# The order of the side steps in the first up stage of a retention and SwiGLU kernel, laid out anew

## The chip, the core and the metric

The kernel runs on one core of one Trainium2 chip. The metric is the device time of one execution in microseconds (us); the number for a kernel is the median of several executions. Five engines work side by side on the core, each through its own list of instructions in order: TensorE (PE in the profile), VectorE (DVE), ScalarE (ACT), GpSimd (POOL), and SyncE (SP), which here only issues transfers (DMA). An instruction that has to wait holds up everything behind it in the list of its own engine.

## What is computed

```python
# retention, for B=4 sequences, H=8 heads, S=768 tokens, head size D=64
for t in range(S):
    state = gamma * state + k[t] (outer) v[t]
    y[t]  = scale * q[t] @ state
x = y as (3072 tokens, 512)
# SwiGLU block, d_ff = 1536
g   = x @ w_gate
val = x @ w_val
out = (silu(g) * val) @ w_out
```

The three weight matrices arrive as 8-byte words, so the kernel first turns them into 4-byte floats. This can be seen in the sizes of the loads: the 512 x 256 values that one step of the up stage needs come as 1 MB.

## The kernel before, in words

The 3072 tokens are taken in four segments of 768 (two sequences, three chunks of 128 tokens each). Each segment has an up stage, in which both `x @ w_gate` and `x @ w_val` are formed, and a down stage, which multiplies by `w_out`. The retention of the first segment comes before everything (the string `START`); that of each later segment is woven into the down stage before it. The hidden dimension of 1536 is cut into 12 blocks of 128, counted by f.

**The first up stage** is what the change is about: `up(f)`, lines 654 to 702, called for f = 0 to 11. The gate and value blocks are treated as one 2 x 2 block product and formed with seven products where eight would be plain, each of 128 x 384 results and two contracted blocks (line 664, two full-precision matmuls, four records in the trace). For this, weights and inputs are first added and subtracted. For one f the list of PE is:

- B11 into bank x (bank 0 for even f, 1 for odd f), then T4 of the f before into the other x bank (`gates`, line 673), then T1 into bank 2, T2 into x, B22 into bank 2, T3 into x, B21 into bank 3.
- ACT copies x after B11 (line 683), runs the two Silu of the f before (lines 675 and 676), copies bank 2 after T1 (line 688) and x after T2 (line 691). B22 and T3 add to what stands in their banks and therefore wait for these copies.
- DVE adds after B22 (line 694), after T3 (line 697) and after B21 (line 700). The addition of line 697 reads x, so T4 of this f, which adds to x in the next f, waits for it. `muls` (lines 679 and 680) multiply by the gate and free the x bank for the f after next.

**The side steps.** Between these products the kernel prepares the weights for later f and for the down stage, and stores them in DRAM for the segments to come. The list `beside`, indexed by `6 * f + place`, is the table of places: `aside(f, place)` issues the steps written there. Place 0 stands after T4, place 1 after T1 and its copy, 2 after T2 and its copy, 3 after B22 and its addition, 4 after T3 and its addition, 5 after B21 and its addition. Nothing but this table (and waits on data) decides where a side step stands in the list of its engine. `START` is such a list for the work ahead of f = 0. The letters, with n the number of a weight piece (0 to 11: up, block f = n; 12 to 23: down, blocks 3 to 11 and then 0, 1, 2):

- `Un:w` loads a piece into raw space w (SP, line 191; three transfers for an up piece, 1 MB, one for a down piece, 512 KB). Raw space: `rawp0` to `rawp3` hold one up piece or two down pieces each, the front of `loads` two down pieces more.
- `an`, `cn`, `bn` convert on ACT: a (line 209) the upper words, c (line 217) the lower words, b (line 213) the signs into PSUM banks, two of 512 columns for an up piece and one for a down piece. `Sn` (DVE, line 223) joins signs and words, `Cn` (POOL, line 232) adds the lower words. Cn needs Sn and cn; Sn needs bn.
- `Tn:0`, `Tn:1`, `Tn:2` (DVE, line 80) form T1 and T3, T2, and T4 of up piece n; Tn:0 needs Cn.
- `Fn:0` to `Fn:3` split a down piece into three parts of lower precision: ACT (line 728), POOL (line 731), DVE (line 734), DVE (line 738). The parts lie in one of three slots.
- `Zn` stores a prepared piece (SP, line 160 for up, 249 for down), `Mf` is `muls` of f, `Ln` and `Pn` load tables and q, k, v for the later retention (SP; L is four or five small transfers), `gn` decays a retention state (ACT, four instructions, line 445), `tn`, `kn` work on the state and on k.

The list of SP is in order too. Each transfer waits, besides for its data, for the one issued eight before it to have landed, since eight counters are used in turn.

**Later stages.** `WHEN` holds times at which steps of the other stages are issued in program order; `('u', 0)` to `('u', 3)` are those of `up3`, the up stage of segments 1 to 3, for f = 0, 1, 2 to 10, and 11.

Of the kernel before, what the change touches and what calls it, by code (L numbers as in the profile page):

```python
# [24 lines left out]
NF = DFF // P  # L25
L = 3
TH = L * P
NSEG = B * NCK // (2 * L)
# [21 lines left out]
def tile_retnet_swiglu(  # L50
# [69 lines left out]
    def at(t, fn, *args, **kw):  # L120
        events.append((t, len(events), lambda: fn(*args, **kw)))
# [30 lines left out]
    T3, B22, B12, T1, B11, B21, T2, T4 = 0, 1, 2, 2, 3, 4, 5, 6  # L152
# [131 lines left out]
    def do(order):  # L284
        for o in order.split():
# [6 lines left out]
        l0:0 l0:1 A0 A1 l1:0 l1:1 l0:2 l1:2 A2 l0:3 l2:0 l2:1 l1:3 l2:2 l2:3 l3:0 l3:1 l3:2  # L292
        l3:3 l4:0 l4:1 U0:0 l4:2 l5:0 l5:1 l5:2 U1:2 l4:3 l5:3 s0 w6 s1 m0 m1 K0 t0 K1 s2 t1
        g2 g3 Q2 s3 m2 x0:0 x0:1 x0:2 x0:3 k2 q3 t2 s4 a0 b0 m3 k3 t3 q4 c0 s5 S0 x1:0 x1:1
        x1:2 x1:3 m4 a1 q5 C0 U2:0 m5 x2:0 T0:0 x2:1 T0:1 x2:2 x2:3 T0:2 U3:4 U12:6
    """
    beside = """
        b1 | c1 S1 U13:7 | g5 g4 C1 | a2 T1:0 U14:8 | U15:9 | c2 b2 T1:1 a3 |
        S2 T1:2 | b3 C2 Z0 S3 | Z1 T2:0 | c12 c3 a12 C3 M0 b12 | U5:0 a13 T2:1 | T2:2 |
        S12 C12 T3:0 M1 |  | T3:1 F12:0 U4:2 Z2 | T3:2 a4 b4 U6:4 S4 a5 Z3 | F12:1 c4 F12:2  # L300
            C4 | b5 S5 T4:0 |
        T4:1 c6 L0 | M2 U16:6 c5 C5 | b13 c13 S13 | L1 C13 U7:2 a6 a14 | F12:3 T5:0 U8:0 b6
            | T4:2 T5:1 S6 F13:0 |
        F13:1 Z4 F13:2 b14 | F13:3 Z13 C6 M3 S14 | a15 a7 b7 c7 | T5:2 T6:0 T6:1 Z12 | S7
            T6:2 Z5 L3 c14 b15 | C14 U18:8 F14:0 |
        S15 C7 F14:1 | M4 F14:2 F14:3 | a8 U9:4 U17:7 Z6 c15 | C15 a16 Z14 | L2 F15:0 T7:0 |
            F15:1 c8 b8 |
        T7:1 S8 | U10:2 F15:2 a9 M5 C8 F15:3 | a17 T7:2 c16 b16 | U19:9 T8:0 b9 | U11:0 S16
            P0 C16 S9 F16:0 | P1 b17 |
        F16:1 T8:1 F16:2 Z15 c9 | T8:2 F16:3 Z7 | a10 Z16 S17 c10 C9 | c17 M6 C17 | U22:4  # L310
            a19 U20:6 F17:0 T9:0 a18 F17:1 | T9:1 b10 |
        k4 Z8 U21:7 b18 | S10 C10 a11 F17:2 S18 | M7 U23:5 c18 F17:3 | T10:0 T9:2 | b19 Z9
            b11 C18 F18:0 | T10:1 F18:1 F18:2 S11 P2 c19 Z17 c11 |
        T10:2 S19 F18:3 M8 a20 | b20 C11 | c20 S20 | a21 b21 T11:0 | a22 S21 C19 C20 | T11:1
            T11:2 t4 c21 Z18 F19:0 |
        F19:1 F19:2 k5 F20:0 Z10 F19:3 | b22 F20:1 t5 C21 a23 b23 | F21:0 S22 c22 M9 F21:1
            Z11 F20:2 | c23 F20:3 C22 Z19 | S23 F22:0 C23 F21:2 | F21:3 Z20 |
        F23:0 F22:1 Z21 F22:2 | M10 F22:3 Z22 | F23:1 F23:2 |  | F23:3 | |
        Z23
    """.split("|")  # L320
    sign_banks = {0: (0, 1), 1: (4, 5), 3: (4, 6), 12: (7,), 19: (4,), 20: (7,), 21: (6,), 22: (7,), 23: (6,), 4: (6, 7), 5: (6, 7), 6: (6, 7), 7: (6, 7), 8: (6, 7), 9: (6, 7), 10: (6, 7), 11: (6, 7), 13: (4,), 14: (4,), 15: (4,), 16: (4,), 17: (4,), 18: (4,), 2: (6, 7)}

# [2 lines left out]
    WHEN = {  # L325
        ('u', 0): (1.15, 2.16, 2.86, 3.39, 4.9, 5.3, 8.05, 13.63, 7.4, 8.1),
        ('u', 1): (0.41, 2.51, 3.16, 3.92, 4.38, 5.59, 6.95, 8.3, 7.26, 12.66),
        ('u', 2): (0.33, 1.32, 3.61, 3.15, 4.0, 5.51, 5.85, 6.13, 7.28, 7.66),
        ('u', 3): (1.63, 1.81, 3.34, 2.86, 3.53, 5.07, 6.18, 7.14, 7.05, 7.54),
        ('w', 0, 0): (-11.39, -6.27, -4.75),  # L330
        ('w', 0, 1): (-7.89, -7.84, -1.53),
        ('w', 0, 2): (-10.42, -10.31, -9.95),
        ('w', 1, 0): (-9.1, -4.79, -3.1),
# [47 lines left out]
        'end': (1.36, -0.0, 0.1, 1.03, 7.96, 4.59),  # L381
        'last': (0.1, 0.1, 0.1, 0.1, 0.1, 0.1),
        ('h', 12): (-7.5, -6.3, -5.3),
    }

    UP0, T0 = 9.45, 18.0
# [420 lines left out]
    def weights(t, f, g):  # L807
        it = {}

        def begin():  # L810
            it["o"] = group(f, g)
            near_a(*it["o"])

        a, b, c = WHEN["w", min(f, 2), g]
        at(t + a, begin)
        at(t + b, lambda: near_b(*it["o"]))
        at(t + c, lambda: near_c(it["o"][0]))
# [11 lines left out]
    def up3(s, f, t):  # L829
        x, z, wb = (banks[i][:, :TH] for i in (6 + f % 2, 0, 1))  # L830
        p1, u2, p5 = (tmp[:, ts(i, TH)] for i in range(3))
        c11 = tmp[:, ts(3 + f % 2, TH)]
        gate = banks[2 + f % 2][:, :TH]
        for g, first in enumerate((0, 3, 6)):
            weights(t + first * PROD, f, g)
        for n, p in enumerate(ORDER):
            o = {1: x, 6: x, 7: x, 4: x, 2: z, 5: wb, 3: wb}[p]
            at(t + n * PROD, product, s, f, p, o, p in (1, 2, 5))
        h0, h1 = hT[:, f, 0], hT[:, f, 1]
        steps = (lambda: copy(p1, x), lambda: tt(c11, z, p1, op=add),  # L840
                 lambda: act(gate, c11, AF.Silu, scale=ONE), lambda: copy(u2, x),  # L841
                 lambda: copy(p5, wb), lambda: tt(h1, x, p5, op=add),  # L842
                 lambda: tt(h0, wb, u2, op=add), lambda: tt(h0, h0, gate, op=mul),  # L843
                 lambda: act(x, x, AF.Silu, scale=ONE), lambda: tt(h1, h1, x, op=mul))  # L844
        for d, step in zip(WHEN["u", 3 if f == NF - 1 else min(f, 2)], steps):
            at(t + d, step)


# [144 lines left out]
    for s in range(1, NSEG):  # L993
        for f in range(NF):
            up3(s, f, t + UPT * f)
            if f > 2:
                at(t + UPT * (f - 1) - 2.5, load_unit, f)
        t += NF * UPT
        if s + 1 < NSEG:
            for n in range(5):  # L1000
                at(t - (18, 13, 12, 5, 4)[n], load_pair, s + 1, n)
        t = down_stage(s, t)
# [52 lines left out]
```

## Time and profile before

| what | value |
|---|---|
| three executions | 674.3, 675.67, 678.9 us; median 675.67 us |
| profiled execution, its own time | 674.72 us |
| span from its first to its last instruction | 672.9 us |
| granted TensorE clock, mean | 0.997 |
| PE busy in the span | 658.1 us (98%) |
| DVE, ACT, POOL busy | 466.1, 386.7, 250.5 us |
| first up stage in the trace | about 29.5 to 149 us |
| engines busy from 40 to 150 us (110 us) | PE 105.4, DVE 92.2, ACT 82.3, POOL 59.9 us |

The share of a stage in a time is read from the trace in order of time. A row of the timeline has the start, the length from the first start to the last end, the engine, the line of the kernel, what is written and read, the count, and in brackets the idle time of the engine before the row with what ended it. Matmul rows of the first up stage have line 664; the additions on DVE are lines 694, 697 and 700.

### The profile page before, as it was taken

What the parts mean: (1) busy time and instruction counts of PE and PEld (TensorE: products, weight loads), DVE (VectorE), ACT (ScalarE), POOL (GpSimd) and SP (SyncE); (2) the same over time, 40 slices, a digit from 0 to 9 for tenths busy, and PEclk for the clock granted to TensorE, in tenths of its full rate; (3) what the DMA queues carried; (4) which work ended last, traced back from release to release, by engine and by line L of the source; (5) the groups of instructions that cost most, each with busy time, mean ns of one, the idle gap of its engine ahead of it and who ended that gap; (6) DMA issues with size and microseconds to landing.
All of it is one profiled execution on the core that took longest, in us unless ns stands there. A gap on an engine that the chain in (4) does not pass through costs nothing.

```text
span 672.9 us, 12402 instructions
## 1 busy us (share of the span) xinstructions
PE 658.1 (98%) x4724; PEld 548.8 (82%) x4724; DVE 466.1 (69%) x742; ACT 386.7 (57%) x793; POOL 250.5 (37%) x164
## 2 busy tenths in 40 slices
PE   8998899999999999999998999999999999999997
PEld 7754455567778999997776999998777899999886
DVE  3766988986777766666687676666776776667541
ACT  3587769756647656555748655556474755554221
POOL 0444546640103566550100665562010655653000
PEclk9999999999999999999999999999999999999999
DMA  9798999967685533465765443374766454323553
GB/s 315 265 374 306 337 319 403 374 232 211 227 260 210 193 122 110 156 204 183 257 219 196 162 153 110 110 221 163 240 220 221 176 180 145 130 64 134 187 188 141
DMA packets 49723, 141.59 MB, mean 210 GB/s; under 512 B 6144, under 2 KB 18944, under 8 KB 49664
## 3 DMA queue, kind: packets, MB, share of 16 engines
q1 hardware_dynamic: 49664, 140.80, 60.4%
q8 instruction: 37, 0.61, 0.4%
q14 instruction: 22, 0.18, 0.1%
HBM read 114.04 MB, written 26.74 MB: 209 GB/s over the span
## 4 chain that ended last, share of the span: by engine, by line
PE 85%; DMA 7%; DVE 3%; ACT 3%; issue 1%; POOL 1%; SPq 0%; DVEq 0%; ACTq 0%; POOLq 0%
PE bank L825 39%; PE bank L875 28%; PE bank L664 10%; PE bank L521 6%; DMA loads<-wup 1%; DMA rawp<-in_q_t_dram 1%; DMA rawp<-in_w_gate_dram 1%; DVE first L80 1%; DMA rawp<-in_w_val_dram 1%; DMA hT<-in_k_n_dram 1%; DMA hT<-in_k_t_dram 1%; ACT rawp L217 1%; DMA tab<-in_decays_dram 1%; POOL gitem L725 1%; DVE oitem L738 0%
## 5 line engine op out<-in xcount | busy, mean ns | idle before, releaser
L825 PE MATMUL bank<-x,gitem 128*128 128x384 f32 x1296 | 231.8, 335 | 0.1
L825 PEld LDWEIGHTS bank<-x,gitem 128*128 128x128 f32 x1296 | 225.8, 188 | 1.2 <-POOL gitem L725 0.4
L875 PE MATMUL bank<-oitem,gitem 128*128 128x512 f32 x864 | 214.8, 401 | 0.2 <-DVE hT L843 0.2
L875 PEld LDWEIGHTS bank<-oitem,gitem 128*128 128x128 f32 x864 | 158.7, 188 | 40.9 <-issue 2.9
L725 POOL TENSOR_TENSOR gitem<-gitem 128x768 fp32r<-128x768 f32 x72 | 138.6, 1946 | 119.0 <-DVE gitem L722 112.5
L664 PE MATMUL bank<-first 128*128 128x384 f32 x336 | 112.9, 495 | 5.0 <-DVE hT L697 3.7
L664 PEld LDWEIGHTS bank<-first 128*128 128x128 f32 x336 | 63.5, 192 | 52.5 <-DVE hT L697 4.9
L719 ACT ACTIVATE gitem<-loads 128x768 fp32r<-128x768 f32 x72 | 57.9, 840 | 36.4 <-issue 30.8
L594 POOL TENSOR_TENSOR loads<-loads,tab 128x512 f32<-128x512 f32 x8 | 12.7, 1591 | 142.7 <-PE bank L521 142.7
L722 DVE SCALAR_TENSOR_TENSOR gitem<-gitem,loads 128x768 fp32r<-128x768 f32 x72 | 65.5, 951 | 0.0
L719 ACT ACTIVATE gitem<-hT 128x768 fp32r<-128x768 f32 x48 | 40.1, 840 | 36.7 <-PE bank L875 24.5
L722 DVE SCALAR_TENSOR_TENSOR gitem<-gitem,hT 128x768 fp32r<-128x768 f32 x48 | 45.9, 960 | 18.1 <-ACT gitem L719 18.0
L232 POOL TENSOR_TENSOR first<-first,rawp 128x1024 int32<-128x1024 int32 (+1 forms) x21 | 41.4, 1973 | 36.4 <-ACT rawp L217 14.2
L80 DVE SCALAR_TENSOR_TENSOR gitem<-gitem 128x768 fp32r<-128x768 f32 x48 | 46.0, 963 | 0.8
L760 ACT COPY chunk_x<-bank 64x256 f32<-64x256 f32 x72 | 25.6, 368 | 34.8 <-PE bank L521 34.1
L841 ACT COPY tmp<-bank 128x384 f32<-128x384 f32 x36 | 17.2, 479 | 46.3 <-PE bank L825 44.6
L825 PE MATMUL bank<-x,oitem 128*128 128x384 f32 x216 | 43.8, 338 | 0.0
L725 POOL TENSOR_TENSOR oitem<-oitem 128x256 fp32r<-128x256 f32 x36 | 28.6, 794 | 29.5 <-DVE oitem L722 27.2
L842 DVE TENSOR_TENSOR hT<-bank,tmp 128x384 f32<-128x384 f32 x36 | 20.1, 558 | 27.1 <-PE bank L825 27.1
L844 DVE TENSOR_TENSOR hT<-hT,bank 128x384 f32<-128x384 f32 x36 | 19.9, 553 | 26.8 <-ACT bank L844 26.8
L825 PEld LDWEIGHTS bank<-x,oitem 128*128 128x128 f32 x216 | 38.0, 188 | 0.0
L840 DVE TENSOR_TENSOR tmp<-bank,tmp 128x384 f32<-128x384 f32 x36 | 20.1, 557 | 19.2 <-PE bank L825 19.2
(93 smaller groups left out, 726.2 us busy)
## 6 DMA issues: line engine op xcount, KB each, us to landing
oitem<-wdnt SPq DMA_DIRECT2D x45, 768.0 KB, 4.3
loads<-wup SPq DMA_DIRECT2D x36, 896.0 KB, 4.9
wup<-first SPq DMA_DIRECT2D x12, 896.0 KB, 7.7
wdnt<-oitem SPq DMA_DIRECT2D x12, 768.0 KB, 5.0
rawp<-in_w_val_dram SPq DMA_DIRECT2D x24, 256.0 KB, 6.5
rawp<-in_w_gate_dram SPq DMA_DIRECT2D x12, 512.0 KB, 7.2
out_dram<-chunk_x SPq DMA_DIRECT2D x24, 256.0 KB, 2.1
loads<-in_k_t_dram SPq DMA_DIRECT2D x18, 256.0 KB, 3.4
```

What stands on the lines that cost most here:

```text
L80: stt(o, x, 1.0, y, op0=mul, op1=op)
L232: pool(d[:, ts(i, n)].bitcast(I32), d[:, ts(i, n)].bitcast(I32), lo[:, ts(i, n)].bitcast(I32), op=add)
L521: nc.tensor.matmul(o, a, b, start=start, stop=True, skip_group_check=True)
L664: nc.tensor.matmul(o, w[:, slot, k], a[:, k], start=(start and k == 0), stop=(stop and k == KH - 1), skip_group_check=True)
L719: act(o[0], x, AF.Copy, scale=CUT / FAR)
L722: stt(o[1], f32(o[0]), -FAR, x, op0=mul, op1=add)
L725: op(o[2], f32(o[0]), f32(o[1]), op=add)
L760: copy(cx[half[i], ds(2 * h, 2), c], y_both(h, i, c))
L825: nc.tensor.matmul(o, w[:, a, k], xs_of[s][:, a, OP[p], k], start=start and a == k == 0, stop=a == 2 and k == KH - 1, skip_group_check=True)
L840: steps = (lambda: copy(p1, x), lambda: tt(c11, z, p1, op=add), lambda: act(gate, c11, AF.Silu, scale=ONE), lambda: copy(u2, x), lambda: c ...
L842: lambda: copy(p5, wb), lambda: tt(h1, x, p5, op=add),
L875: nc.tensor.matmul(banks[tok], hs[f][:, a, ds(i * TH + u * P, P)], wo[f][:, a], start=f == a == 0, stop=f == NF - 1 and a == 2, skip_group ...
```

## The change

Only tables are edited. The place in `beside` is new for 185 of the 261 steps that stay in it, for most by one to four places; one load (`U15:9`) moves from the table into `START`, ahead of `U3:4`. A tuple `('u', 4)` with the ten numbers of `('u', 3)` is added to `WHEN`, and `up3` takes it for the last f of the last segment. No step is added or left out, and no data, size or bank changes.

```diff
@@ -292,31 +292,31 @@
         l0:0 l0:1 A0 A1 l1:0 l1:1 l0:2 l1:2 A2 l0:3 l2:0 l2:1 l1:3 l2:2 l2:3 l3:0 l3:1 l3:2
         l3:3 l4:0 l4:1 U0:0 l4:2 l5:0 l5:1 l5:2 U1:2 l4:3 l5:3 s0 w6 s1 m0 m1 K0 t0 K1 s2 t1
         g2 g3 Q2 s3 m2 x0:0 x0:1 x0:2 x0:3 k2 q3 t2 s4 a0 b0 m3 k3 t3 q4 c0 s5 S0 x1:0 x1:1
-        x1:2 x1:3 m4 a1 q5 C0 U2:0 m5 x2:0 T0:0 x2:1 T0:1 x2:2 x2:3 T0:2 U3:4 U12:6
+        x1:2 x1:3 m4 a1 q5 C0 U2:0 m5 x2:0 T0:0 x2:1 T0:1 x2:2 x2:3 U15:9 T0:2 U3:4 U12:6
     """
     beside = """
-        b1 | c1 S1 U13:7 | g5 g4 C1 | a2 T1:0 U14:8 | U15:9 | c2 b2 T1:1 a3 |
-        S2 T1:2 | b3 C2 Z0 S3 | Z1 T2:0 | c12 c3 a12 C3 M0 b12 | U5:0 a13 T2:1 | T2:2 |
-        S12 C12 T3:0 M1 |  | T3:1 F12:0 U4:2 Z2 | T3:2 a4 b4 U6:4 S4 a5 Z3 | F12:1 c4 F12:2
-            C4 | b5 S5 T4:0 |
-        T4:1 c6 L0 | M2 U16:6 c5 C5 | b13 c13 S13 | L1 C13 U7:2 a6 a14 | F12:3 T5:0 U8:0 b6
-            | T4:2 T5:1 S6 F13:0 |
-        F13:1 Z4 F13:2 b14 | F13:3 Z13 C6 M3 S14 | a15 a7 b7 c7 | T5:2 T6:0 T6:1 Z12 | S7
-            T6:2 Z5 L3 c14 b15 | C14 U18:8 F14:0 |
-        S15 C7 F14:1 | M4 F14:2 F14:3 | a8 U9:4 U17:7 Z6 c15 | C15 a16 Z14 | L2 F15:0 T7:0 |
-            F15:1 c8 b8 |
-        T7:1 S8 | U10:2 F15:2 a9 M5 C8 F15:3 | a17 T7:2 c16 b16 | U19:9 T8:0 b9 | U11:0 S16
-            P0 C16 S9 F16:0 | P1 b17 |
-        F16:1 T8:1 F16:2 Z15 c9 | T8:2 F16:3 Z7 | a10 Z16 S17 c10 C9 | c17 M6 C17 | U22:4
-            a19 U20:6 F17:0 T9:0 a18 F17:1 | T9:1 b10 |
-        k4 Z8 U21:7 b18 | S10 C10 a11 F17:2 S18 | M7 U23:5 c18 F17:3 | T10:0 T9:2 | b19 Z9
-            b11 C18 F18:0 | T10:1 F18:1 F18:2 S11 P2 c19 Z17 c11 |
-        T10:2 S19 F18:3 M8 a20 | b20 C11 | c20 S20 | a21 b21 T11:0 | a22 S21 C19 C20 | T11:1
-            T11:2 t4 c21 Z18 F19:0 |
-        F19:1 F19:2 k5 F20:0 Z10 F19:3 | b22 F20:1 t5 C21 a23 b23 | F21:0 S22 c22 M9 F21:1
-            Z11 F20:2 | c23 F20:3 C22 Z19 | S23 F22:0 C23 F21:2 | F21:3 Z20 |
-        F23:0 F22:1 Z21 F22:2 | M10 F22:3 Z22 | F23:1 F23:2 |  | F23:3 | |
-        Z23
+        U14:8 c1 b1 | S1 | g4 C1 a2 T1:0 |  | c2 | g5 U13:7 T1:1 b2 |
+        S2 a3 Z0 | T1:2 b3 Z1 C2 | S3 T2:0 U5:0 a12 | c3 M0 a13 | T2:1 | b12 c12 S12 |
+        C3 U4:2 | T3:0 C12 a5 T2:2 | M1 F12:0 T3:1 L0 | a4 b4 | U6:4 S4 c4 | b5 S5 T3:2
+            F12:1 C4 T4:0 |
+        Z2 c6 | U7:2 c5 T4:1 | T4:2 F12:2 a14 M2 b13 | U16:6 S13 L1 c13 | C5 a6 T5:0 b14
+            T5:1 C13 | b6 a15 F13:0 |
+        Z3 F12:3 S6 F13:1 L3 C6 | U8:0 F13:2 M3 S14 | T5:2 T6:0 Z12 a7 Z4 | b7 c7 | T6:1
+            F13:3 Z13 U9:4 c14 C14 T6:2 | b15 F14:0 S7 |
+        U17:7 F14:1 C7 M4 U10:2 | S15 Z6 | F14:2 F14:3 a8 |  | T7:0 Z5 c15 C15 b8 Z14 |
+            F15:0 c8 U19:9 |
+        S8 a16 F15:1 L2 | U18:8 F15:2 c16 M5 b16 C8 F15:3 T8:0 S16 | a9 a17 C16 |  | T7:1
+            U11:0 b9 T7:2 U20:6 | S9 F16:0 T8:1 F16:1 T8:2 |
+        P1 c9 | b17 | F16:2 c17 C9 F16:3 P2 a18 Z15 M6 | S17 a10 b10 a19 T9:0 C17 Z7 F17:0 |
+            k4 U23:5 | c10 Z16 b18 |
+        U22:4 F17:1 | T9:1 S10 T9:2 S18 M7 C10 | c18 C18 U21:7 F17:2 | T10:0 P0 c11 T10:1
+            b19 | F18:0 F17:3 a11 Z17 | F18:1 b11 Z9 F18:2 S11 |
+        a21 S19 c19 | Z8 F18:3 C11 M8 | t4 c20 a20 Z18 b20 | T11:0 b21 C19 S20 | k5 F19:0
+            a23 c21 T11:1 F19:1 | T10:2 c22 Z10 S21 a22 C20 T11:2 c23 |
+        F19:2 F20:0 F20:1 F19:3 M9 | F20:2 F20:3 C21 Z19 | b22 S22 b23 t5 F21:0 S23 | Z20
+            F21:1 | F21:2 C22 C23 Z11 | F22:0 F22:1 |
+        F23:0 F21:3 F22:2 | F23:1 M10 F22:3 | Z22 |  |  | F23:2 F23:3 Z23 Z21 |
+        
     """.split("|")
     sign_banks = {0: (0, 1), 1: (4, 5), 3: (4, 6), 12: (7,), 19: (4,), 20: (7,), 21: (6,), 22: (7,), 23: (6,), 4: (6, 7), 5: (6, 7), 6: (6, 7), 7: (6, 7), 8: (6, 7), 9: (6, 7), 10: (6, 7), 11: (6, 7), 13: (4,), 14: (4,), 15: (4,), 16: (4,), 17: (4,), 18: (4,), 2: (6, 7)}
 
@@ -381,6 +381,7 @@
         'end': (1.36, -0.0, 0.1, 1.03, 7.96, 4.59),
         'last': (0.1, 0.1, 0.1, 0.1, 0.1, 0.1),
         ('h', 12): (-7.5, -6.3, -5.3),
+        ('u', 4): (1.63, 1.81, 3.34, 2.86, 3.53, 5.07, 6.18, 7.14, 7.05, 7.54),
     }
 
     UP0, T0 = 9.45, 18.0
@@ -842,7 +843,7 @@
                  lambda: copy(p5, wb), lambda: tt(h1, x, p5, op=add),
                  lambda: tt(h0, wb, u2, op=add), lambda: tt(h0, h0, gate, op=mul),
                  lambda: act(x, x, AF.Silu, scale=ONE), lambda: tt(h1, h1, x, op=mul))
-        for d, step in zip(WHEN["u", 3 if f == NF - 1 else min(f, 2)], steps):
+        for d, step in zip(WHEN["u", 3 + (s == NSEG - 1) if f == NF - 1 else min(f, 2)], steps):
             at(t + d, step)
 
 
```

## Prediction

> **What bounds the kernel now.** I read the page first, then the waits of PE and its timeline through the first up stage, then what DVE, ACT and POOL did just before each gap.
>
> ```profile
> span 672.9 us, 12402 instructions
> ...
> L664 PE MATMUL bank<-first 128*128 128x384 f32 x336 | 112.9, 495 | 5.0 <-DVE hT L697 3.7
> ```
>
> PE is busy 98% of the span, and the stage concerned has 336 records. The PE timeline shows their pace and gaps:
>
> ```profile
> 42.62 15.79 PE L664 MATMUL bank<-first 128*128 128x384 f32 x48 [0.63 <-ACT tmp L683]
> 59.83 4.14 PE L664 MATMUL bank<-first 128*128 128x384 f32 x12 [1.42 <-DVE hT L697]
> 64.26 14.58 PE L664 MATMUL bank<-first 128*128 128x384 f32 x44 [0.30 <-ACT tmp L688]
> ...
> 81.11 5.18 PE L664 MATMUL bank<-first 128*128 128x384 f32 x10 [2.27 <-DVE hT L697]
> ```
>
> Forty-eight records in 15.79 us: 0.3225 from start to start, so a product (4 records) is 1.29 us. Ten records take 5.18 us after the longest gap; the windows table says why (last columns: granted clock, DMA share, GB/s):
>
> ```profile
> 81.00:86.00 5.00, 4.89 (x10) 2.79 (x11) 3.67 (x8) 1.52 (x4) 3.62 (x2) 0.66 0.83 264
> ```
>
> Start to start minus 0.3225, the stage loses: at 31.40, 0.73; at 42.62 (T2 of f=1), 0.90; at 59.83 (T4 of f=2), 1.69; at 64.26 (B22 of f=3), 0.66; at 81.11 (T4 of f=4), 2.53 plus five records of 0.645 and some ends, 4.22 in all; small ones 0.6. Together 8.8 us: the most that new places can give back. From 85.5 on PE hardly waits. What stood before the two large gaps, DVE, then POOL:
>
> ```profile
> 58.02 1.29 DVE L223 SCALAR_TENSOR_TENSOR first<-first,bank 128x512 uint32<-128x512 uint32 x2 [2.11 <-ACT bank L213]
> 59.22 0.55 DVE L697 TENSOR_TENSOR hT<-bank,tmp 128x384 f32<-128x384 f32 x1
> ...
> 73.71 2.53 DVE L738 TENSOR_SCALAR oitem<-oitem 128x512 fp32r<-128x512 f32 x1
> 78.16 2.43 DVE L80 SCALAR_TENSOR_TENSOR first<-first 128x256 f32<-128x256 f32 x3
> 80.51 0.55 DVE L697 TENSOR_TENSOR hT<-bank,tmp 128x384 f32<-128x384 f32 x1
> ```
> ```profile
> 73.21 2.74 POOL L232 TENSOR_TENSOR first<-first,rawp 128x1024 int32<-128x1024 int32 x1 [1.94 <-DMA rawp<-in_w_val_dram]
> 78.69 1.61 POOL L232 TENSOR_TENSOR first<-first,loads 128x512 int32<-128x512 int32 x1 [2.74 <-ACT loads L217]
> ```
>
> First gap: S4 stands on DVE ahead of the line 697 addition of f=2 and waits for b4, which waits on ACT for the load of piece 4, landed at 56.05. Second: F13:3 (2.53 us) and T6:1 (1.39 of the 2.43) are ahead of the line 697 addition of f=4, each ending with a POOL operation.
>
> [...]F:3 takes 0.43 us with POOL idle (86.82) and 2.53 against POOL. [...]a store that waits holds up loads behind it; the SyncE waits agree (line 160 waits 25.7 us in all for DVE line 80).
>
> **The change, part by part.** The new tuple of WHEN repeats the old numbers: 0. No step is added, so the engines' work stays and only its order counts. Durations from the timelines: a and c of an up piece 1.04, b two times 0.52, of a down piece 0.57 and 0.52; S 1.2 or 0.6; T:0 0.6; T:1, T:2 0.34; copies and Silu 0.4; lines 694, 697, 700 0.47; M 0.93; F:0 0.55, F:2 0.6, F:3 0.41; C 2.4 or 1.28; F:1 1.27; g 1.0.
>
> *START and f=0.* U15 ahead of U3 puts 0.5 MB, 1.3 us, before piece 3 (landing 42.1 instead of 40.8); a3 comes later anyway. c1 before b1 delays S1 by nothing, since DVE was busy till 32.9 (S1 33.05 to 34.25); C1 keeps 34.4. The T1:0 moved ahead of the line 694 addition waits for C1 (36.8); 694 then ends at 37.9, line 697 at 38.4, before T4 needs it at 39.2. Cost 0.
>
> *f=1: a loss.* ACT before: a2 c2 b2 a3, copy at 42.1. After: a2 c2 g5 b2, copy: g5 (1.0) replaces a3 (1.04), so the 0.90 stays. But a3 now follows the Silu and comes ahead of the copy of line 688, which moves from 43.27 to 44.31 and ends at 44.8; B22 would start at 44.01. PE loses 0.84 + 0.10. b3 then ends at 45.74, the copy of line 691 at 46.2, T3 is due at 46.25: nothing more. **+0.94.** f=2 then starts at 48.8 instead of 47.9; M0 ends at 48.5.
>
> *f=2: the first large gap goes.* ACT: a5 moves ahead of the copy of line 691 and waits for piece 5. The transfers ahead of it are the same and the queue is backed up without a break, so it lands at 53.3 again: a5 to 54.4, copy to 54.8, T3 due at 55.3. Then a4 (load 56.05) 57.1, b4 58.15. S4 now stands behind line 697, which follows T3 (55.3 to 56.75) and ends at 57.25. T4 of f=2 is due at 59.2: no wait. **-1.69.** Late next is C4 (59.25 to 61.65), and with it T4:0 on DVE; f=4 needs it at 67.
>
> *f=3.* c6 goes ahead of the copy of line 688, as before, so it must have piece 6. The five small loads of L0 now stand ahead of U6 on SP, and each transfer waits for the eighth before it: the last part of U6 goes at 56.1 (when U4 has landed), not 52.25. It lands 3.2 us later at best (31.07 to 34.27 in an empty queue), 6.3 at worst (31.58 to 37.85): 59.3 to 62.4; before 61.0. c6 is due at 61.4, B22 at 63.1, so the cost is 0 to 0.9; I take 0.3. It replaces 0.66. **-0.36.**
>
> *f=4 and 5: the second large gap.* DVE from 63.3: F12:2, M2, 694, S13, 697 of f=3 end at 66.4. C13 follows C5 on POOL with no break (66.35 to 67.6) and holds T5:0 till then; T5:0, T5:1, 700, F12:3, S6 to 70.65. F13:2 waits for F13:1 (70.95)[...]; F13:2 74.0, M3 74.95 (B11 of f=5 due at 76.0), S14, T5:2, T6:0 76.5, 694, 697 of f=4 at 77.45. T4 is due at 77.3. F13:3 and T6:1 now come after. Residue 0.15 + 0.1; bounds 0[...] and 1.5 (C14 ahead of T6:0), too short to halve the clock by the 1.4 us case above. I take 0.3. **-3.92.**
>
> *f=6 to 11.* DVE has, per f, 4.5, 8.3, 4.6, 8.6, 6.5, 6.5 us of work for f=5 to 10 against 9.03 of PE; line 697 keeps 1.7 to 2 us of slack. Loads of pieces 7 to 11 land over 5 us ahead of their a; stores of split parts leave each slot 7 us or more before its next use. POOL is busy 7.9 of ten at most (110 to 120). Cost 0, covered by that slack; without it each lost us is a us. The small 0.6 stays.
>
> Sum: +0.94 - 1.69 - 0.36 - 3.92 = -5.03. The chain behind the stage is PE almost throughout and its orders are unchanged, so it moves along. Span 672.9 - 5.0 = 667.9; the execution's own 674.72 becomes 669.7. The median of the runs is 0.95 above that execution: **670.7 us**.
>
> **Rivals.**
> 1. *The second gap stays.* Speaks for it: my DVE walk leaves no slack at f=4[...]. Over 2 us of further holding bring back the gap and the half clock: of 3.9 at least 2.4 is lost, 673 to 675 us.
> 2. *More goes.* Only f=0's 0.73 and some 1.0 of small losses stay, if c6 and F13:2 are lucky and a3 slips in elsewhere: 8.8 - 1.7 = 7.1 gained, 668.6 us. Against it: a3's place is in the list.
> 3. *Slower: ACT held by a load.* c6 at f=3 waits for U6, with two copies and thus PE behind it. From 61.7 on each us of lateness is a us; at about 67.1 the gain is gone, at 74 the kernel is 1% slower. Against it: the queue landed nothing over 13.3 us after issue, mostly 6 to 8. It gives 677 to 686 us.
> 4. *No effect*: the time is regained by a later transfer that has its own clock. Against it: loads of the down stage land by then or depend on PE. 675 us.
>
> **Numbers.** Forecast (669 to 672.5) 0.56, rival 1 0.2, rival 2 0.09, rival 3 0.1, rival 4 0.05. The range 668 to 675.2 takes in the forecast with rivals 1 and 4 and the nearer part of rival 2; it leaves out rival 3 and the rest of rival 2, under 2 in 10. About 1% (6.8 us) is what a measurement of this kernel tells from no change. Faster by more, below 668.9: rival 2 and the forecast's rim, 0.13; slower by more, above 682.4: half of rival 3, 0.05; within: 0.82.
>
> **What would show it.** Right: no gap at T4 of f=2; a gap of 0.4 to 0.5 before B22 of f=1 waiting for line 688; clock full from 76 to 86; T4 of f=4 near 77.4; the stage ending 5 us earlier. Wrong: a gap over 2 us at f=4 or later, a wait of line 217 for a load at 61 that lasts, or DVE falling behind at f=6 or 8, the heavy ones.

## The result and the profile after

| | before | after |
|---|---|---|
| median of 20 executions each (us) | 675.46 | 677.16 |
| lowest and highest (us) | 672.92, 679.28 | 674.91, 680.96 |
| profiled execution, its span (us) | 674.72, 672.9 | 678.09, 676.3 |
| first up stage in the profile, first product to the end of B21 of f=11 (us) | 117.5 | 119.2 |

The ratio after to before is 1.0026 (1.0012 to 1.004): 1.7 us slower, a small difference but a clear one, where 5.0 us less was forecast. The lines behind the added tuple are one higher than before: the matmuls of the stage have line 665, the copies 684, 689 and 692, the addition after T3 698. From the page:

```profile
span 676.3 us, 12404 instructions
...
L665 PE MATMUL bank<-first 128*128 128x384 f32 x336 | 113.1, 492 | 6.4 <-ACT tmp L684 3.6
```

The matmuls take about the same time; the idle time before them grew from 5.0 to 6.4 us, and its largest releaser is no longer DVE (3.7 us for the addition) but a copy on ACT. The timeline of PE through the stage, kernel after (start, length, engine, what, count, idle time before the row and what ended it):

```profile
44.26 17.17 PE L665 MATMUL bank<-first 128*128 128x384 f32 x52 [0.65 <-ACT tmp L689]
61.87 1.56 PE L665 MATMUL bank<-first 128*128 128x384 f32 x4 [0.44 <-ACT tmp L684]
64.09 17.25 PE L665 MATMUL bank<-first 128*128 128x384 f32 x52 [0.67 <-ACT tmp L689]
81.68 9.30 PE L665 MATMUL bank<-first 128*128 128x384 f32 x28 [0.34 <-ACT tmp L684]
91.28 1.56 PE L665 MATMUL bank<-first 128*128 128x384 f32 x4 [0.30 <-ACT tmp L684]
93.02 8.18 PE L665 MATMUL bank<-first 128*128 128x384 f32 x24 [0.18 <-ACT tmp L689]
103.26 1.56 PE L665 MATMUL bank<-first 128*128 128x384 f32 x4 [2.06 <-ACT tmp L684]
105.46 4.78 PE L665 MATMUL bank<-first 128*128 128x384 f32 x14 [0.65 <-ACT tmp L689]
```

Both gaps of before are gone: the row from 44.26 runs past T4 of f=2, that from 64.09 to 81.34 past T4 of f=4. Every gap in these rows is ended by ACT. DVE in the kernel after shows that the additions did move up: that of f=2 ends at 56.87, well before T4; F13:3 comes after the addition of f=4 and takes 0.42 us instead of 2.53, with no POOL operation beside it (the next one starts at 79.10):

```profile
56.31 0.56 DVE L698 TENSOR_TENSOR hT<-bank,tmp 128x384 f32<-128x384 f32 x1 [0.67 <-PE bank L665]
...
77.89 0.54 DVE L698 TENSOR_TENSOR hT<-bank,tmp 128x384 f32<-128x384 f32 x1
...
78.69 0.42 DVE L739 TENSOR_SCALAR oitem<-oitem 128x512 fp32r<-128x512 f32 x1
```

Where did it go? f=6 begins at 86.94 instead of 90.65, so 3.7 us were gained by then. From T2 of f=5 to T2 of f=8 the kernel after loses 6.3 us (start to start minus 0.3225, as in the prediction; 0.6 in f=5, 1.2 in f=6, 3.2 in f=7, 1.3 in f=8), where before lost 0.3. f=12 would begin at 149.16 instead of 147.50: the stage loses 10.5 us in all against 8.8. ACT in the kernel after:

```profile
75.07 1.16 ACT L209 ACTIVATE first<-rawp 128x1024 f32<-128x1024 f32 x1 [1.04 <-DMA wup<-first]
...
86.05 1.16 ACT L209 ACTIVATE first<-rawp 128x1024 f32<-128x1024 f32 x1 [2.30 <-DMA wup<-first]
...
99.59 1.70 ACT L209 ACTIVATE first<-rawp 128x1024 f32<-128x1024 f32 x2 [5.16 <-DMA wup<-first]
...
102.73 0.47 ACT L684 COPY tmp<-bank 128x384 f32<-128x384 f32 x1
```

These are a7, a8 and a9 (with a17). They wait neither for their load nor for another engine but for `wup<-first`: a store of an up piece. The reason is in the code, in a line that the prediction did not read: the prepared up pieces lie in four places in turn.

```python
wt[f] = ring[f % 4].rearrange("p (a b) -> p a b", a=7)
```

So the a of piece n overwrites piece n-4 and has to wait until Z of piece n-4 has **landed**. ACT's list is in order: behind a9 stand a17, b9, F16:0 and the copy of line 684 at 102.73, and PE's T2 waits for that copy (2.06 us idle at 103.26). The waits of ACT at line 209 that the profile puts down to these stores, first the kernel after, then before (total, times, longest):

```profile
ACT first L209 <- DMA wup<-first: 8.5, 3, 5.2
```
```profile
ACT first L209 <- DMA wup<-first: 1.9, 1, 1.9
```

The three waits of the kernel after end within 0.2 us of the landing of Z3, Z4 and Z5. The single one of before is a4 at 56.21, and there the profile names the wrong transfer: no store landed between 50.2 and 58.2, but the last part of the load of piece 4 did, at 56.05. Before did not wait for a store at all.

| store | landed before | landed after | the a that needs its place, before | after |
|---|---|---|---|---|
| Z3 | 63.2 | 75.0 | a7 at 74.7 | a7 at 75.1 |
| Z4 | 78.7 | 85.9 | a8 at 87.4 | a8 at 86.1 |
| Z5 | 84.5 | 99.6 | a9 at 95.1 | a9 at 99.6 |

Of 8.7 to 11.5 us of slack nothing was left. Two things stand behind this. The table puts Z3 at 24 (before: 15) and Z5 at 34 (before: 28). And SP had a hole. SP and then POOL, kernel after:

```profile
57.37 0.45 SPq L160 DMA_DIRECT2D wup<-first  x1
62.91 0.88 SPq L191 DMA_DIRECT2D rawp<-in_w_val_dram  x2
...
69.31 0.52 SPq L160 DMA_DIRECT2D wup<-first  x1
```
```profile
60.48 2.40 POOL L232 TENSOR_TENSOR first<-first,rawp 128x1024 int32<-128x1024 int32 x1 [4.06 <-DMA rawp<-in_w_gate_dram]
```

The load of piece 7 overwrites the raw words of piece 4, so it waits for C4 (60.48 to 62.88), and from 57.8 to 62.9 SP issues nothing, though U16 and L1 stand behind it with nothing to wait for (e6, below, issues them first). The last transfer in flight lands at 63.2. So everything behind this load on SP starts late, Z3 among it. The windows tables (stretch, length, busy time and count of PE, PEld, DVE, ACT, POOL, then clock, share of the DMA engines and GB/s), first after, then before:

```profile
55.00:60.00 5.00, 5.00 (x17) 2.88 (x17) 2.27 (x4) 3.00 (x5) 1.27 (x1) 1.00 0.95 207
60.00:65.00 5.00, 3.90 (x12) 1.87 (x11) 4.61 (x9) 5.00 (x10) 2.40 (x1) 1.00 0.66 257
```
```profile
55.00:60.00 5.00, 3.58 (x12) 1.88 (x11) 2.89 (x6) 3.76 (x5) 0.64 (x1) 1.00 1.05 401
60.00:65.00 5.00, 4.70 (x14) 2.51 (x15) 3.99 (x8) 5.00 (x9) 2.40 (x1) 1.00 0.82 259
65.00:70.00 5.00, 5.00 (x17) 2.80 (x16) 4.03 (x7) 5.00 (x10) 3.67 (x3) 1.00 0.60 142
```

By 60 us the kernel after had moved 18.5 MB, before 19.7 (sum of the transfers' records). These 1.2 MB are not a debt that stays: the kernel before has a slack stretch of its own from 60 to 70 us, and the kernel after is 0.65 MB behind at 70 us, 1.7 at 80, 0.3 at 100 and 0.95 at 125 (40.86 against 41.81), where its stage is late itself. What the hole costs has to be read from the transfers that stand behind it on SP, and not from the sum of the bytes.

Last, the two spans differ by 3.4 us, the medians by 1.7. The stage gives 1.7 of the 3.4. Another 2.0 arise in the second down stage (0.3 are regained behind it), where both kernels have a gap behind ACT, and the kernel after also a stretch of half clock behind it (365.06 to 368.47 us). The profiles of this study, which have one order of work there, show that stage between 70.3 and 75.0 us long, so a single profile decides nothing on that part. Before, then after:

```profile
362.39 1.15 PE L521 MATMUL bank<-loads 128*64 128x64 f32 x32 [1.84 <-ACT chunk_x L760]
```
```profile
364.60 1.63 PE L522 MATMUL bank<-loads 128*64 128x64 f32 x32 [2.32 <-ACT chunk_x L761]
```

### The profile page after: what moved, and what is told of

It reads as the page before. It is cut to its first block, busy times and chain, and to the rows that moved or that the text cites. A ratio compares the mean times of both kernels' runs of the same rounds, so it can differ in the third digit from the quotient of the medians.

```text
span 676.3 us, 12404 instructions
## 1 busy us (share of the span) xinstructions
PE 659.7 (98%) x4724; PEld 549.1 (81%) x4724; DVE 470.0 (69%) x742; ACT 386.6 (57%) x793; POOL 249.4 (37%) x164
## 4 chain that ended last, share of the span: by engine, by line
PE 81%; DMA 9%; ACT 3%; DVE 2%; issue 2%; POOL 1%; SPq 1%; POOLq 0%; DVEq 0%; ACTq 0%
PE bank L826 39%; PE bank L876 30%; PE bank L522 6%; PE bank L665 5%; DMA rawp<-in_w_val_dram 2%; DMA rawp<-in_w_out_dram 1%; DMA kept_vk<-in_decays_dram 1%; POOL first L232 1%; DMA rawp<-in_q_t_dram 1%; DMA hT<-in_k_n_dram 1%; DMA rawp<-in_w_gate_dram 1%; DMA wup<-first 1%; DMA hT<-in_k_t_dram 1%; SPq L191 1%; ACT bank L213 1%
## 5 line engine op out<-in xcount | busy, mean ns | idle before, releaser
L723 DVE SCALAR_TENSOR_TENSOR gitem<-gitem,hT 128x768 fp32r<-128x768 f32 x48 | 45.8, 960 | 18.5 <-ACT gitem L720 18.5
L232 POOL TENSOR_TENSOR first<-first,rawp 128x1024 int32<-128x1024 int32 (+1 forms) x21 | 40.5, 1936 | 30.1 <-DVE first L223 15.2
L603 ACT ACTIVATE loads<-loads,tab 128x64 f32<-128x64 f32 x112 | 27.8, 334 | 11.3 <-PE bank L522 8.0
```

The source lines that it names most:

```text
L232: pool(d[:, ts(i, n)].bitcast(I32), d[:, ts(i, n)].bitcast(I32), lo[:, ts(i, n)].bitcast(I32), op=add)
L603: act(kd[:, h], kd[:, h], AF.Copy, scale=dec[:, ds(h, 1)])
L723: stt(o[1], f32(o[0]), -FAR, x, op0=mul, op1=add)
```

## The experiments

Three theories. **S**: the late stores alone cost it, each through its ring place. **Q**: the queue as a whole runs behind after the hole, and whatever is put ahead in it makes another transfer late. **D**: the gains on DVE and ACT were never there. The expectations of e2, e3 and e4 also name **P**: DVE is slowed by GpSimd's operations beside its own (F13:3: 2.53 us in before, 0.42 after), and the gaps stay where they are. Diffs show the rows of `beside` by number. All kernels of a table ran beside the kernel before on the same chip. Their tables take fewer lines: in e2, e3, e5, e6, e7, e11 and e12 matmuls are line 659 and the copies 678, 683, 686; in e4, e8, e9, e10, e13 it is 658 and 677, 682, 685.

### First group: stores earlier, and the gains alone

*e2: after, with Z5 right behind Z4.*

```diff
@@ 26 @@
-T5:2 T6:0 Z12 a7 Z4
+T5:2 T6:0 Z12 a7 Z4 Z5
@@ 34 @@
-T7:0 Z5 c15 C15 b8 Z14
+T7:0 c15 C15 b8 Z14
```

> The changed kernel with one step moved: the store of up piece 5 (Z5) from place 34 to place 26, behind Z4. Theory S (stores): piece 9 is converted into the ring slot that piece 5 leaves, so a9 on ACT waits until Z5 has landed (99.6 us in the changed kernel) and holds the copy of line 684 behind it. Then a9 starts near 94.5, the gaps of f=7 (2.3 before T2, 0.9 before B22) and the 1.2 of f=8 go, and the kernel takes some 3.5 us less than the changed one, about 0.997 of before. Theory Q (the queue is full): from 80 us on the transfers are at their limit, what moves ahead pushes the loads back, a9 waits for the load of piece 9 instead, and the time stays at 1.0026. Theory P[...]: DVE is behind because of GpSimd; the gaps stay where they are, 1.0026.

*e3: after, with Z3, Z4 and Z5 all early.*

```diff
@@ 18 @@
-Z2 c6
+Z2 Z3 c6
@@ 20 @@
-T4:2 F12:2 a14 M2 b13
+T4:2 Z4 F12:2 a14 M2 b13
@@ 24 @@
-Z3 F12:3 S6 F13:1 L3 C6
+F12:3 S6 F13:1 L3 C6
@@ 26 @@
-T5:2 T6:0 Z12 a7 Z4
+T5:2 Z5 T6:0 Z12 a7
@@ 34 @@
-T7:0 Z5 c15 C15 b8 Z14
+T7:0 c15 C15 b8 Z14
```

> The changed kernel with three stores moved: Z3 from place 24 to 18, Z4 from 26 to 20, Z5 from 34 to 26. Theory S: besides a9, a7 (75.1, when Z3 had landed) and a8 (86.1, Z4) are no longer held; of the 6.3 us lost in f=5 to f=8 at least 5 come back: 0.9945 to 0.996 of before. Theory Q: the loads of pieces 7, 8 and 9 land later by the bytes put ahead of them (0.9 MB, 2.3 us each) and the sum is little changed: 1.001 to 1.003. Theory P: 1.0026.

*e4: before, with only the moves that should close the two large gaps.*

```diff
@@ 15 @@
-T3:2 a4 b4 U6:4 S4 a5 Z3
+T3:2 a4 b4 U6:4 a5 Z3
@@ 16 @@
-F12:1 c4 F12:2 C4
+S4 F12:1 c4 F12:2 C4
@@ 25 @@
-F13:3 Z13 C6 M3 S14
+C6 M3 S14
@@ 27 @@
-T5:2 T6:0 T6:1 Z12
+T5:2 T6:0 Z12
@@ 28 @@
-S7 T6:2 Z5 L3 c14 b15
+F13:3 Z13 S7 T6:1 T6:2 Z5 L3 c14 b15
```

> The kernel before with only the moves that took its two large gaps away: S4 from place 15 to 16, F13:3 (with its store Z13) from 25 to 28, T6:1 from 27 to 28. If the gain of the change was real and only given back by its late stores, the gaps at T4 of f=2 (1.7) and of f=4 (4.2 with the half clock) go and nothing new comes, since the stores stay early: 0.992 to 0.994 of before. If any earlier PE runs into side work that cannot keep up (theories Q and P), new gaps of the same sum come up at f=6 to f=8: 0.999 to 1.002.

*e5: e3, and g5 out of the way of f=1.*

```diff
@@ 5 @@
-g5 U13:7 T1:1 b2
+U13:7 T1:1 b2
@@ 10 @@
-T2:1
+T2:1 g5
```

> As the run with Z3, Z4 and Z5 earlier, and g5 (1.0 us on ACT) from place 5 to place 10, where ACT waits for PE anyway. The copy of line 684 of f=1 is then 1.0 earlier, and the 0.92 before B22 of f=1 shrinks to 0.1 or so: 0.9 us below the run without this move, 0.993 to 0.995 of before. If the early loss is taken up by a later wait for a transfer at f=2 or 3, the two runs are the same.

| kernel | median us | before us | ratio (95%) |
|---|---|---|---|
| e2 | 677.95 | 675.58 | 1.0031 (1.0011 to 1.0051) |
| e3 | 679.74 | 675.58 | 1.007 (1.0043 to 1.0096) |
| e4 | 674.76 | 675.58 | 0.998 (0.9961 to 0.9999) |
| e5 | 677.53 | 675.58 | 1.0036 (1.0017 to 1.0054) |

In e2 the gap of f=7 went and another came. PE, then ACT, in e2:

```profile
125.76 2.52 PE L659 MATMUL bank<-first 128*128 128x384 f32 x7 [2.67 <-ACT tmp L683]
```
```profile
124.13 0.66 ACT L209 ACTIVATE first<-rawp 128x512 f32<-128x512 f32 x1 [3.29 <-DMA rawp<-in_w_out_dram]
```

ACT waits again for a transfer, two f later, but for a load of `w_out`: S alone falls, and so does P, since the gap of f=7 went. In e3 the loads behind the stores are late instead, and it is the slowest of the four (six executions). Waits of ACT in e3, 80 to 130 us:

```profile
ACT first L209 <- DMA rawp<-in_w_out_dram: 3.5, 1, 3.5
ACT first L209 <- DMA rawp<-in_w_gate_dram: 2.0, 1, 2.0
```

e5 lies 0.0034 below e3, but their intervals overlap (1.0043 and 1.0054), and its profile still loses 0.7 us at B22 of f=1: that g5 set the place of that copy isn't shown. e4 keeps before's stores and no longer has the two large gaps, so D falls too. It gains 0.2% where 0.6 to 0.8 were expected, because new waits came. PE waits from 29 to 150 us and ACT, in e4:

```profile
PE bank L658 <- ACT tmp L677: 1.8, 1, 1.8
PE bank L658 <- ACT tmp L685: 1.4, 1, 1.4
```
```profile
112.54 1.13 ACT L209 ACTIVATE first<-rawp 128x1024 f32<-128x1024 f32 x1 [1.45 <-DMA wup<-first]
```

The first is at f=3, where a4, which waits for its load, and a5 stand ahead of the copy; the second is at f=8, behind a11, which waits for Z7 (the row of ACT). The stage that comes earlier itself uses up the store's slack: Z7 lands at 112.5 as before (113.0), but ACT comes to a11 at 111.1 and not at 113.8.

### Second group: is it the queue?

*e6: after, with U16 and L1 ahead of the load that waits for C4.*

```diff
@@ 18 @@
-Z2 c6
+Z2 U16:6 L1 c6
@@ 21 @@
-U16:6 S13 L1 c13
+S13 c13
```

> The changed kernel with two steps moved: U16 (0.5 MB) and L1 from place 21 to place 18, ahead of U7. In the changed kernel U7 stands on SP from 57.8 to 62.9 waiting for C4, with nothing in flight from 63.2 on and 1.2 MB less moved by 60 us than before. Theory Q, sharpened (what counts is the bytes moved by a given time; the queue is full from 80 to 135 us, so an early hole is never made up): the hole is filled with 0.5 MB, worth 1.3 us at 400 GB/s, and with the issue of five small transfers; the later gaps shrink by that much: 1.5 us under the changed kernel, 1.0003 of before. If only the place of single stores counts[...]: 1.0026 as for the changed kernel.

*e7: after with e6's move of U16, and all tables at the end of the stage: L0 and L1 at 60, L2 and L3 at 61. e8: the kernel before with all tables there; its rows (each L is gone from its old place):*

```diff
@@ 60 @@
-F19:1 F19:2 k5 F20:0 Z10 F19:3
+F19:1 F19:2 k5 F20:0 Z10 F19:3 L0 L1
@@ 61 @@
-b22 F20:1 t5 C21 a23 b23
+b22 F20:1 t5 C21 a23 b23 L2 L3
```

> The changed kernel with U16 ahead of U7 and all four table loads L0 to L3 (18 small transfers, needed only from 150 us on) at places 60 and 61. Theory Q: SP no longer spends issue time and turns of its eight counters on them between 48 and 95 us, U6, U7 and U8 are issued earlier and a7, a8, a9 are no longer held: of the 6.3 us lost in f=5 to f=8 at least 4 come back, 0.994 to 0.997 of before. If bytes alone count (the tables have 0.8 MB in all) 2 us come back, 0.9995. If transfers are not the bound: 1.0026.

> The kernel before with L0 to L3 at places 60 and 61 and nothing else. Its two large gaps have other causes (S4 behind a load[...]), so by theory Q little is gained here, 0.5 to 1 us: 0.9985 to 1. If the table loads are what holds the kernel in general: 0.994.

*e9: e4, with a5 moved from 15 to 13 (ahead of the copies of f=2) and the tables as in e8.*

> The kernel before with S4, F13:3 (with Z13) and T6:1 behind the additions as in the run of three moves, a5 at place 13 as in the changed kernel (which takes 1.04 us of ACT from in front of the copy of line 684 of f=3, where that run had a gap of 1.9), and L0 to L3 at places 60 and 61. By theory Q both the order on DVE and the feeding of the queue are right here: of 8.8 us lost some 3 are left, 0.991 to 0.993 of before. If PE ahead of its side work always runs into new gaps: 0.998, as the run of three moves.

| kernel | median us | before us | ratio (95%) |
|---|---|---|---|
| e6 | 674.48 | 675.60 | 0.9987 (0.9963 to 1.001) |
| e7 | 682.18 | 675.60 | 1.0115 (1.0086 to 1.0144) |
| e8 | 680.50 | 675.60 | 1.0097 (1.0067 to 1.0127) |
| e9 | 678.39 | 675.60 | 1.0045 (1.0028 to 1.0063) |

e6 moves two steps and is 0.0039 below the change. Its windows, PE and ACT:

```profile
60.00:65.00 5.00, 4.44 (x14) 2.38 (x13) 4.59 (x8) 5.00 (x10) 2.39 (x1) 1.00 0.99 347
```
```profile
83.66 15.64 PE L659 MATMUL bank<-first 128*128 128x384 f32 x48
101.43 10.74 PE L659 MATMUL bank<-first 128*128 128x384 f32 x27 [2.14 <-ACT tmp L678]
```
```profile
97.78 1.68 ACT L209 ACTIVATE first<-rawp 128x1024 f32<-128x1024 f32 x2 [5.44 <-DMA wup<-first]
```

From 60 to 65 us it moved 347 GB/s instead of 257, and what stands behind on SP comes earlier: Z3 and Z4 are issued at 66.45 and 73.94 us (69.31 and 76.56 in the kernel after) and land at 73.4 and 82.9 (75.0 and 85.9). a7 and a8 no longer wait; the losses of f=5 and f=6 are gone. What stays is Z5 at place 34. So two causes add up: the hole for a7 and a8, the late place for a9. e6 moves more bytes and brings single transfers forward at once, so by itself it does not tell the two apart.

e7 and e8 were meant to take 18 small transfers out of the busy stretch. They only moved the trouble: in e8 the 18 transfers hold SP from 123.4 to 137.0 us. PE and ACT in e8:

```profile
143.89 6.60 PE L658 MATMUL bank<-first 128*128 128x384 f32 x14 [4.01 <-ACT tmp L677]
```
```profile
ACT oitem L722 <- DMA wdnt<-oitem: 8.2, 1, 8.2
```

The stores of the split parts queue behind the tables, an F on ACT waits 8.2 us for its slot, and the copy behind it for the F. e9 loses about 5 us up to f=10, where 3 were expected for the whole stage, and 6 at f=11 for the same reason.

### Third group: put together

*e10: e9 with the tables spread out (the rows against those of the kernel before). e13: the same four moves with the tables where before has them.*

```diff
@@ 61 @@
-b22 F20:1 t5 C21 a23 b23
+b22 F20:1 t5 C21 a23 b23 L0
@@ 64 @@
-S23 F22:0 C23 F21:2
+S23 F22:0 C23 F21:2 L1
@@ 65 @@
-F21:3 Z20
+F21:3 Z20 L2
@@ 66 @@
-F23:0 F22:1 Z21 F22:2
+F23:0 F22:1 Z21 L3 F22:2
```

> The four moves of the run with tables late, but the table loads in the stretches from 124 to 144 us in which SP waits for DVE anyway: L0 at place 61, L1 at 64, L2 at 65 behind Z20, L3 at 66 behind Z21, four or five transfers at a time. With them in one block, 18 transfers held SP for 14 us and the stores of the split parts behind them, and f=11 lost 6.4 us; up to f=10 that kernel had lost only 4.6. Theory Q with this correction: the loss of f=11 goes, about 5 us are lost in the stage against 8.8, 0.993 to 0.995 of before. If any delay of the stores at the end is too much: a gap at T2 of f=11 again, 1.000 or more.

> The kernel before with S4, F13:3 (and Z13) and T6:1 behind the additions and a5 at place 13; tables where they were. The run of three moves lost 1.9 before T2 of f=3 to a5 on ACT; this one should lose 0.3 there: 1.5 us below it, 0.995 to 0.997 of before. If the time then only passes to a11 waiting for the store of piece 7, which stood at 1.5 us in that run: 0.997 to 0.998.

*e11: e6 and e2 together. e12: e11 with L3 moved from 24 to 62 and L2 from 36 to 66.*

> The changed kernel with U16 and L1 ahead of U7 (the hole on SP filled) and Z5 at place 26. With the hole filled alone, a9 still waited 5.4 us for Z5, and f=7 lost 4.4 with a spell of half clock; with Z5 alone, that gap went but a later load was late and f=9 lost 2.7 instead. If both are needed, as theory Q says, the gap of f=7 goes and none comes for it: 3 us below the kernel with the hole filled, 0.993 to 0.996 of before. If the gap moves on whatever is done (PE ahead of its side work), it comes back at f=8 to f=10: 0.998 to 1.

> As the run with the hole filled and Z5 early, and L3 from place 24 to 62, L2 from 36 to 66. If the turns of small transfers between 70 and 95 us still cost the queue bytes, another 1 us goes: 0.992 to 0.995. If late table loads hold the last stores, f=11 gets a gap: above 0.997.

| kernel | median us | before us | ratio (95%) |
|---|---|---|---|
| e10 | 670.99 | 675.89 | 0.9924 (0.9897 to 0.9951) |
| e11 | 672.91 | 675.89 | 0.9959 (0.994 to 0.9979) |
| e12 | 672.01 | 675.89 | 0.9943 (0.9923 to 0.9962) |
| e13 | 674.06 | 675.89 | 0.9983 (0.9966 to 1.0) |

The change's own order of work, fed better, is faster than before: 1.0026; with the hole filled 0.9987; with Z5 early as well 0.9959; without eight small transfers in the busy stretch 0.9943. The first and the second are told apart by their intervals, as are the first and the third; neighbours among the last three overlap. PE in e11 from 84 us on, then the largest wait of ACT for line 209:

```profile
83.65 36.18 PE L659 MATMUL bank<-first 128*128 128x384 f32 x111
...
122.72 10.99 PE L659 MATMUL bank<-first 128*128 128x384 f32 x28 [2.27 <-ACT tmp L683]
```
```profile
ACT first L209 <- DMA rawp<-in_w_out_dram: 2.9, 1, 2.9
```

One hundred and eleven records without a gap, over the place where the change lost most of its 6.3 us (T2 of f=5, just ahead of them, loses 0.3 instead of 0.6). A load of `w_out` is still late and makes the gap at 122.72, and the 28 records behind it take 10.99 us, 0.39 each against 0.326 in the row above: half clock for some of them, by an estimate from the 0.645 us of a record at half clock in before. Z5 alone gave nothing (e2, 1.0031 beside 1.0026); with the hole filled too the ratio is 0.9959, and e2 and e11 differ by no more than the hole: what an earlier store is worth depends on the rest of SP's list. The sum of the bytes is not what counts: by 80 us e11 had moved 24.4 MB, 0.9 less than the kernel before, and its PE ran on without a gap. The first half of Q, a queue that runs behind as a whole, is not borne out; the second half, that what is put ahead makes another transfer late, is what e2 and e3 show.

e13 has the four moves alone and is no better than e4 (its profile loses 2.0 us at f=8, where a11 waits for Z7); with the tables out of the queue they give 0.9924. This is the lowest median, faster than both kernels; e12's interval overlaps with it. PE in e10:

```profile
54.46 8.01 PE L658 MATMUL bank<-first 128*128 128x384 f32 x24 [0.77 <-ACT tmp L685]
62.75 59.02 PE L658 MATMUL bank<-first 128*128 128x384 f32 x180 [0.28 <-ACT tmp L682]
```

One hundred and eighty records in a row take 59.02 us, 0.328 each; the stage is 112.3 us long. Z3, Z4 and Z5 land at 62.6, 75.2 and 82.3, 6.6 us or more ahead of a7, a8 and a9 (73.2, 81.8, 89.6).

## Why the prediction was wrong

- *START and f=0*: cost 0, and 0.83 us lost against 0.73. Right.
- *f=1, +0.94*: measured 0.92 at B22. T2 kept 0.25 and not 0.90, as the last part of piece 2 landed at 37.3, not 37.85. A little too pessimistic.
- *f=2, -1.69*: right; no gap at f=2.
- *f=3, -0.36*: the last part of U6 landed at 60.98, inside the 59.3 to 62.4, but the steps ahead of the two copies cost 1.7 us at T2 and B22 where 0.3 was taken: a4 to b5 ahead of the first, because the load of piece 4 landed at 56.89 and not at 56.05 again, and c6 ahead of the second. A term that was too small, by 1.4 us.
- *f=4 and 5, -3.92*: right. T4 of f=4 lost 0.08 us where 0.25 to 0.3 was left, and the clock stayed full (1.00 from 81 to 86 us against 0.66). Rival 1 fell. One reservation: 1.6 of the 3.92 is half clock (five records of 0.645 us instead of 0.3225), which the profiled execution of before had behind this gap. Whether other executions had it there was not measured, and by the last section a gap of this length need not bring it, so the term may be too large for the median.
- *f=6 to 11, "Cost 0, covered by that slack"*: this is the step that failed. Its cover was: "Loads of pieces 7 to 11 land over 5 us ahead of their a; stores of split parts leave each slot 7 us or more before its next use". The loads and the slots of the split parts were counted, the ring place that a writes was not. (The part on the loads was too generous as well: those of pieces 7 and 8 landed 4.0 and 4.4 us ahead of their a, late as these were.) The stores of up pieces free it, Z3, Z4 and Z5 had moved back by two to nine places, and 6.3 us were lost there (T2 of f=5, where a7 waits, included). e6 and e11 show that this is the cause: with the hole filled and Z5 early the same order of the engines loses next to nothing there.
- The hole was in reach as well: the walk had the load of piece 7 behind C4, which it put at 59.25 to 61.65, and took it as harmless, because only the lateness of that load was asked for and not what stood behind it on SP. The prediction had read the wait of stores on SP (line 160, 25.7 us in all); the trace of the kernel after shows the same for a load that waits for its buffer: `SPq L191 <- POOL first L232`, 5.0 us at the longest, without an issue.
- *Rival 3* had the right mechanism, ACT held by a transfer with the copies and PE behind it, in the wrong place (the load of piece 6 instead of the stores of pieces 3 to 5). The result lies at the lower end of its 677 to 686. That each us lost in the stage is a us of the kernel fits (the stage is 1.7 us longer, the median too), but one profile of each kernel shows no more than that.
- *Rival 4*: the gain was given back inside the stage. The traces show no transfer with a clock of its own behind it that took it.
- *The clock* does not explain the slower median: the 20 executions of the kernel after had a mean granted clock of 0.9971, those of the kernel before beside the experiments 0.9961 to 0.9965.

What stays open: how much of a remaining microsecond belongs to each of the transfers that are late one after the other in e2, e11 and e13. The stage lengths of single profiles differ from the medians by up to 2 us, and the intervals of e10 and e12 overlap, so which of these is the best stays open as well.

## What to carry to other kernels

For every instruction that moves to another place, list all buffers it writes and what must have let go of them: a buffer that is freed by a store is free when the store has landed, here mostly 6 to 11 us after its issue (median 7.7 in before, 7.9 after), and the wait sits on the engine that writes next (5.16 us on ACT ahead of a9). When a load waits for its buffer on an in-order issuing engine (5.0 us on SP here), ask what stands behind it that could go first, and which buffer each of those will free. A gain in one place brings all later work nearer to its transfers, so it is worth only what their slack allows.

## What the runs showed of the hardware

The clock did not follow the length of a gap. In before it was at half from 81.80 to 85.21 us, 0.7 us behind the end of the gap of 2.27 us; in the kernel after it was at half from 365.06 to 368.47, 0.5 us behind the end of the gap of 2.32 us (364.60): 3.41 us each time. It stayed at 1.00 behind idle times of 1.42 us (before, 59.83), 1.84 (before, 362.39), 2.06 (after, 103.26) and 2.67 (e2, 125.76; full to 128.31, as far as the row below goes). In e6 and e11, behind 2.14 and 2.27 us, the pace of the records tells of half clock, by an estimate: 27 in 10.74 us and 28 in 10.99, where 111 at full pace took 36.18. Before, then e2 (the clock is the third number from the end):

```profile
78.38:81.79 3.41, 1.14 (x4) 0.49 (x3) 3.38 (x6) 1.71 (x4) 1.61 (x1) 1.00 1.02 417
81.80:85.21 3.41, 3.41 (x7) 1.78 (x6) 2.71 (x6) 0.88 (x2) 2.83 (x2) 0.50 0.84 239
```
```profile
121.48:124.89 3.41, 1.60 (x20) 0.79 (x18) 3.17 (x4) 0.76 (x2) 1.63 (x1) 1.00 1.04 424
124.89:128.31 3.42, 2.55 (x8) 1.63 (x9) 0.89 (x2) 3.39 (x8) 2.30 (x2) 1.00 1.03 432
```

In before the gap lies in the first row, and the second, which begins 0.7 us behind it, has half clock. In e2 the second row holds the end of the longer gap and 2.55 us of work behind it, at full clock. What decides between the two was not shown. The half clock of before cost 1.6 us, about as much as the change, and the time of one kernel goes with its mean clock: of 61 executions of the kernel before, the six with a mean clock of 0.999 have a median of 673.7 us, the 31 with 0.997 one of 675.5, the two with 0.990 one of 680.1.

Small transfers held their issuer longer than large ones: 18 tables of mostly 32 or 64 KB held SP for 13.6 us in e8, 0.76 us each (in before most of them took 0.6), while a 256 KB part of a load mostly takes 0.4 to 0.5 us to issue. And the empty queue after the hole helped only the first parts of the load: the two parts of 256 KB landed 2.9 and 3.2 us after their issue (6.3 is the median over the kernel), but the last, 512 KB issued at 63.84, landed at 71.06. That is 7.2 us, the median of such parts (page, part 6), though only its own two 256 KB parts were in flight ahead of it.

SP's eight counters show in both profiles: each tells of 39 of the 312 transfers, and none of the transfers was issued before the one eight ahead of it had landed.
